# The last two output groups of a set-attention and expert kernel are written into transposed-input tiles, under a new order table

## The chip, the cores and the metric

The kernel runs on one core of one Trainium2 chip. The metric is device time of one launch in microseconds (us). Five engines work side by side, each through its own queue in order: TensorE (PE in the profile, with its weight loads as PEld), VectorE (DVE), ScalarE (ACT), GpSimd (POOL) and SyncE (SP), which here issues nearly all DMA transfers. All arrays are float32.

## The reference

Four batches of 11456 tokens of width 128 attend to 32 inducing points, and the tokens then attend to the 32 result rows. The outcome goes through a skip score and an expert layer with a top-1 gate.

```python
def mab(q, kv):
    s = scale * (q @ kv.transpose(0, 2, 1))
    s = s - s.max(-1, keepdims=True)
    a = np.exp(s)
    a /= a.sum(-1, keepdims=True) + 1e-09
    return a @ kv
h = mab(I, x)
out = mab(x, h)
...
e_idx = np.argmax(logits, axis=1)
...
h = np.maximum(xc[mask] @ w1[e], 0.0)
y[mask] = gate_w[mask, None] * (h @ w2[e])
...
out[do_compute] = xc + y
```

Inputs: x (4, 11456, 128), inducing (32, 128), w_skip (128), w_gate (128, 8), w1 (8, 128, 1024), w2 (8, 1024, 128).

## The kernel before, in words

A batch is cut into six groups: five of 2048 tokens and one of 1216 (batch 0 has the short one first). A group lies as four streams of up to 512 tokens, so that the 32 inducing points times four streams fill 128 partitions.

Each batch has two passes and a middle. The **first pass** (`first`) loads a group of x (channels by tokens) over SP, multiplies it by the inducing points (L372), takes running maxima on DVE (L378) and exponentials on ACT (L382), transposes x into token-major tiles `xt` by 128x128 blocks (L407; four blocks a set, copied out of PSUM by ACT at L335 or DVE at L337), transposes the exponentials (L391) and sums the weighted tokens (L417, accumulated at L426). There are two `xt` tiles, each [128, 4, 4, 129] with a column of ones; the first passes of all batches take them in turn. The **middle** makes the 32 rows h of the batch (`hr`, its transpose `hc`, L486 to L512), finds the expert that they go to, fetches that expert's weights over SP (L665, L667: `w1s`, `w2s`), and folds them with h into `yr` (L590, L603, L643, L654). The **second pass** (`second`) scores tokens against `hc` (L693), turns the scores over on DVE (L698), takes maxima (L700), subtracts them (L704), exponentiates (L707), sums (L711), normalises (L716), turns back (L721, `u1`), makes gate values and scales by them (L820, `v`), and turns back again (L721, `u2`). The elementwise steps L704, L716 and L820 may run on POOL or on DVE; a copy out of PSUM may run on ACT or DVE.

`emit` ends a group. It multiplies `u1` by `hr` and `u2` by `yr` into four PSUM banks (L872), copies the four banks into two tiles named `o` of [128, 2, 512] (`stream`, L335 on ACT or L337 on DVE), and SP stores each `o` tile (`store`, L882). There are four `o` tiles in turn: a copy into one waits until its earlier store has landed. At the end of each batch `marking` checks that no token went elsewhere (`lo`, `lom`, `lod`, `lon`, L903 to L936), and `judge` (L957 to L962) joins the marks of all batches into `anyi`, which SP and the other engines read last of all; a further branch for other experts is skipped with these inputs.

The order of all work on all engines comes from a planner that runs when the program is built: each step has a cost for each engine that may run it, the steps and buffers that it needs, and a rank. The table `PLACES` gives each step, by three characters, its rank (two characters) and a surcharge for DVE (one). From these `in_order` picks the next step, its engine and its PSUM bank, and so fixes every engine's queue. In names such as `x_3_4` or `u2_3_4` the first number after the name is the batch, the second the group (0 to 5).

Of the kernel before, what the change touches and what calls it, by code (L numbers as in the profile page):

```python
# [139 lines left out]
def best_order(ops, bufs):  # L140
# [16 lines left out]
    "0f0AP0Cb2913E30CG0D_2ER1CP0FX2E50Aq0Bp09S06v3An07603G42-0AB0Dk0Bm06m0AC0BA04r0BD3Cr38I05N02U4CK02R04013S2Ee05v0AZ06p39B0"
    "9l02f0Aj01s04G0640FB0Cm04c06a0AA3D-46F0Ef0Di09G0Al07X03r2AX01A01x03F33A06J07M20Z02L04o03T02k09o02v00F04k32s15J04h04Q00R0"
    "C603X01N05H03a06800X28M02B04D2BI08_02b08E09001u0AM05K0693BM07I0CY01v46h1Bi0BL4Eu1DJ09k0GX06-07x08t0AD0AV0780EU04X0DL0FS0"
    "6w07u06r13z0AI3DA07e0Cf0Ad0BX07q39-0El04d0Cc02c03803O01q06i02Y19F08R18P07z35u08p14_06s0BB09t0E20440Bf06U2B407H3AR0C54820"  # L160
    "Bx35B08D08S0Fx00o03305C0660D402l27Q07C38N0DO2Cz01X3CL02303k03o0EY06Y0E_07J0Ff05z22_03R0BY05x03v05Z3370FP27D0AJ02100L01Z0"
    "0J05I00l22D0723Ao01K0Dh00x44J02r00601p01n01202T02d01_03205930E03c22X06M02921909v03400-02C02004S24w08H06e01803002504f03D2"
    "1b01W22J07s08l30h08z01130z06g07G01F06y06u09y0BS0A606k42A03p04i23e29h03I17n08O0ES0Cq0GH0D109208q1Be0Bo0FN07m0DS0EE0Da04C0"
    "GG0DT48y0Du0Ae4EB3Cu0Fb3EZ27R0A10E70EW4E40FK0CX4Dd0F809p0GY0DV0Ar0CO0Cl0Cx4Fu2Fl0G409d39s1Fy06246x38u0A-01o08x2A708s0861"
# [981 lines left out]
```

## Time and profile before

| | |
|---|---|
| time before, median of 3 runs | 225.07 us (224.65 to 226.6) |
| profiled execution: its time / its span | 226.54 us / 224.7 us |
| mean granted TensorE clock in it | 0.981 |
| PE busy (matmul) / PEld | 201.1 us (89%) / 116.2 us (52%) |
| DVE / ACT / POOL busy | 170.5 us (76%) / 140.8 us (63%) / 111.0 us (49%) |
| HBM read / written | 27.68 MB / 23.46 MB |

Busy time is the union of an engine's instructions; ends of matmuls are modelled, so a busy PE may hide short stalls. The span runs from the first to the last instruction that the profiler saw, and the run's own time is a little longer. The chain of waits is followed back from the last instruction to what released it.

### The profile page before, as it was taken

The numbers are of one execution on the slowest core, as the hardware profiler recorded it, in microseconds if no ns is written. First come the engines' busy times: TensorE is split into PE (matmuls) and PEld (weight loads), VectorE is DVE, ScalarE is ACT, GpSimd is POOL, SyncE is SP. The second block draws the span as 40 slices with busy tenths as digits, with TensorE's granted clock in tenths as the row PEclk, the third lists the DMA queues.
The fourth block names the chain that finished last, engine by engine and source line by source line (L and its number), as shares of the span: only waits on it lengthen the run. The fifth ranks groups of instructions, "written<-read, shape, count | busy, mean of one in ns | idle before, by whom it ended". The sixth has DMA issues, their size and how long they took to land.

```text
span 224.7 us, 6693 instructions
## 1 busy us (share of the span) xinstructions
PE 201.1 (89%) x2541; PEld 116.2 (52%) x2542; DVE 170.5 (76%) x444; ACT 140.8 (63%) x333; POOL 111.0 (49%) x284
## 2 busy tenths in 40 slices
PE   4899999989999999999999999989999979688630
PEld 1556767657368764543675647327585333233210
DVE  4363653659898997799888787989898989997640
ACT  2356476655598886766996864768785756346730
POOL 7000000222538668457366541357677879989610
PEclk9999999999999999999999999999999999999975
DMA  6999970086796027979993492454221867445692
GB/s 160 378 419 405 412 313 13 6 266 203 248 392 239 3 115 249 297 308 355 370 414 150 190 314 98 141 234 190 93 101 42 330 205 285 190 175 198 252 365 71
DMA packets 16614, 51.64 MB, mean 230 GB/s; under 512 B 1984, under 2 KB 4928, under 8 KB 16576
## 3 DMA queue, kind: packets, MB, share of 16 engines
q1 hardware_dynamic: 16288, 51.12, 61.4%
q8 instruction: 22, 0.36, 0.7%
q14 instruction: 16, 0.13, 0.2%
q10 hardware_dynamic: 288, 0.02, 0.1%
HBM read 27.68 MB, written 23.46 MB: 228 GB/s over the span
## 4 chain that ended last, share of the span: by engine, by line
PE 54%; POOL 11%; DVE 11%; DMA 10%; ACT 5%; issue 4%; SPq 1%; DVEq 0%; ACTq 0%; POOLq 0%
PE bank L407 16%; PE bank L872 12%; PE bank L417 8%; PE bank L372 6%; DMA w1s<-in_w_dram 4%; PE bank L391 3%; DMA x<-in_xT_dram 3%; ACT o L335 3%; PE bank L693 3%; DMA out_dram<-o 3%; POOL e L716 2%; POOL v L820 2%; DVE ts L700 2%; DVE e L698 2%; PE bank L778 2%
## 5 line engine op out<-in xcount | busy, mean ns | idle before, releaser
L407 PE MATMUL bank<-ident,x 128*128 128x128 f32 (+1 forms) x368 | 50.8, 281 | 1.0 <-DMA x<-in_xT_dram 0.8
L335 ACT COPY o<-bank 128x512 f32<-128x512 f32 (+1 forms) x80 | 40.9, 570 | 16.4 <-PE bank L872 14.4
L335 ACT COPY xt<-bank 128x512 f32<-128x512 f32 (+1 forms) x78 | 42.9, 591 | 10.9 <-PE bank L407 10.6
L704 POOL TENSOR_TENSOR e<-e,ts 128x512 f32<-128x512 f32 (+1 forms) x22 | 22.5, 1023 | 49.6 <-DVE cmx L536 37.5
L407 PEld LDWEIGHTS bank<-ident,x 128*128 128x128 f32 (+1 forms) x368 | 40.4, 141 | 12.7 <-issue 3.0
L872 PE MATMUL bank<-u,hr 32*128 32x512 f32 (+1 forms) x192 | 26.0, 608 | 3.4 <-ACT o L335 2.5
L716 POOL TENSOR_TENSOR e<-texp,ts 128x512 f32<-128x512 f32 (+1 forms) x19 | 18.9, 999 | 17.0 <-DVE ts L713 13.0
L820 POOL TENSOR_TENSOR v<-e,gs 128x512 f32<-128x512 f32 (+1 forms) x20 | 20.8, 1040 | 8.9 <-DVE gs L337 4.9
L417 PE MATMUL bank<-xt,a1T 128*32 128x129 f32 (+1 forms) x736 | 25.1, 275 | 0.0
L382 ACT ACTIVATE a<-bank,bias 128x512 f32<-128x512 f32 (+1 forms) x24 | 16.0, 666 | 14.5 <-DVE a L378 14.5
L372 PE MATMUL bank<-x,iT_sb 128*32 128x512 f32 (+1 forms) x192 | 24.8, 583 | 0.0
L872 PE MATMUL bank<-u,yr 32*128 32x512 f32 (+1 forms) x192 | 23.9, 565 | 0.7 <-DVE u L721 0.6
L417 PEld LDWEIGHTS bank<-xt,a1T 128*32 128x32 f32 (+1 forms) x736 | 19.3, 109 | 8.1 <-issue 3.8
L693 PE MATMUL bank<-x,hc 128*32 128x512 f32 (+1 forms) x192 | 22.8, 573 | 0.1
L707 ACT ACTIVATE texp<-e 128x512 f32<-128x512 f32 (+1 forms) x24 | 14.6, 609 | 10.9 <-POOL e L704 8.0
L378 DVE TENSOR_SCALAR_CACHE_REDUCE a<-bank,bias 128x512 f32<-128x512 f32 (+1 forms) x20 | 13.9, 693 | 5.5 <-PE bank L372 5.2
L698 DVE STREAM_TRANSPOSE e<-bank 128x512 f32<-128x512 f32 (+1 forms) x24 | 15.9, 664 | 2.1 <-PE bank L693 2.0
L721 DVE STREAM_TRANSPOSE u<-v 128x512 f32<-128x512 f32 (+1 forms) x24 | 15.9, 664 | 1.7 <-POOL v L820 1.6
L721 DVE STREAM_TRANSPOSE u<-e 128x512 f32<-128x512 f32 (+1 forms) x24 | 15.6, 661 | 1.1 <-POOL e L716 0.9
L700 DVE TENSOR_REDUCE ts<-e 128x16 f32<-128x512 f32 (+1 forms) x24 | 15.7, 653 | 0.8
L711 DVE TENSOR_REDUCE sums<-texp 128x16 f32<-128x528 f32 (+1 forms) x24 | 15.6, 648 | 0.9 <-ACT texp L707 0.9
L872 PEld LDWEIGHTS bank<-u,yr 32*128 32x128 f32 x192 | 9.8, 185 | 10.8 <-issue 5.8
(153 smaller groups left out, 293.9 us busy)
## 6 DMA issues: line engine op xcount, KB each, us to landing
x<-in_xT_dram SPq DMA_DIRECT2D x43, 512.0 KB, 8.1
out_dram<-o SPq DMA_DIRECT2D x40, 512.0 KB, 3.9
out_dram<-o SPq DMA_DIRECT2D x8, 304.0 KB, 4.7
w1s<-in_w_dram SPq DMA_DIRECT2D x4, 512.0 KB, 4.2
w2s<-in_w_dram SPq DMA_DIRECT2D x4, 512.0 KB, 4.9
x<-in_xT_dram SPq DMA_DIRECT2D x4, 152.0 KB, 2.8
x<-in_xT_dram SPq DMA_DIRECT2D x3, 96.0 KB, 9.1
iT_sb<-in_iT_dram ACTq DMA_DIRECT2D x1, 16.0 KB, 2.2
```

The source lines that it names most:

```text
L335: nc.scalar.copy(out=out, in_=in_)
L372: nc.tensor.matmul(ps[q * M:(q + 1) * M, 0:W], lhsT=iT_sb, rhs=s.x[g][:, G.s1[q]:G.s1[q] + W], start=True, stop=True)
L407: nc.tensor.transpose(out=px[0:w, q * P:(q + 1) * P], in_=s.x[g][:, o:o + w], identity=ident)
L417: nc.tensor.matmul(ph[q * M:(q + 1) * M, 0:P + 1], lhsT=st["aT"][0:w, i, q * M:(q + 1) * M], rhs=xts[bx.idx][0:w, i, q, :], start=(i == 0) ...
L693: nc.tensor.matmul(ps[q * M:(q + 1) * M, 0:W], lhsT=s.hc[:, 0:M], rhs=x()[:, G.s2[q]:G.s2[q] + W], start=True, stop=True)
L698: nc.vector.transpose(out=t[:, 0:W], in_=st["ps"][:, 0:W])
L700: nc.vector.tensor_reduce(out=mx[:, 0:nb], in_=blocks(t), axis=AX.X, op=ALU.max)
L704: on(o).tensor_tensor(out=blocks(t), in0=blocks(t), in1=wide(st["mx"]), op=ALU.subtract)
L716: on(o).tensor_tensor(out=blocks(st["e"]), in0=ev(M), in1=wide(st["i"]), op=ALU.mult)
L721: nc.vector.transpose(out=st[f"u{k}"][:, 0:W], in_=st[src][:, 0:W])
L820: on(o).tensor_tensor(out=blocks(u), in0=blocks(st["e"]), in1=wide(st["gm"]), op=ALU.mult)
L872: nc.tensor.matmul(bank(bp[q].idx)[:, 0:G.w1], lhsT=m[r, :], rhs=st[k][r, c], start=(k == "u1"), stop=(k == "u2"))
```

## The change

It has two parts. In the last batch, the last two groups in number (g = 4 and g = 5) no longer take `o` tiles: group 4 copies its four banks into `xt1` and group 5 into `xt0`, each seen as two halves of 1024 columns, and the stores read from there. These two groups neither take nor free an `o` buffer in the planner. And every character of `PLACES` is replaced, so that every queue stands in another order and some steps run on another engine. All computed operations and their sizes stay.

```diff
 PLACES = (
-    "6f04O07A08w08i07W4EO0Au2CN0BE07Z09L0CF0Dj0GS0Fj04V0BK09N0881AW0BU0EL06z4Fr0FV37b0As0BP02a06H00304q02F06Q05F23V01Q18B0603"
...
+    "Db08q0CS0Bv0G30Gr4GD0A839f0GL3GT0ES0FC09y07X08R0Bl06P09E0DY45904H43K04x12Y0A_14A03e23H05s04d07Z02w04l02Z03t46y04G0A403O4"
...
+        late = b == B - 1 and NG - g <= BUFS["xt"]
+
         def stream(o, q):
-            if q % 2 == 0:
+            if late:
+                v = xts[NG - 1 - g].rearrange("p i q c -> p (i q c)")
+                t[q // 2] = v[:, q // 2 * (GC // 2):(q // 2 + 1) * (GC // 2)].rearrange("p (q w) -> p q w", q=2)
+            elif q % 2 == 0:
                 t[q // 2] = wk.tile([P, 2, GC // Q], F32, tag="o", bufs=BUFS["o"], name=f"o_{b}_{g}_{q // 2}")
             copy(o, t[q // 2][:, q % 2, 0:G.w1], bank(bp[q].idx)[:, 0:G.w1])
...
-            o = L.add({**act(G.w1), **dve(G.w1)}, lambda o, q=2 * h: stream(o, q), m, o, take=[bo], free=[bp[2 * h]])
+            o = L.add({**act(G.w1), **dve(G.w1)}, lambda o, q=2 * h: stream(o, q), m, o, take=[] if late else [bo], free=[bp[2 * h]])
             p = L.add({**act(G.w1), **dve(G.w1)}, lambda o, q=2 * h + 1: stream(o, q), o, free=[bp[2 * h + 1]])
-            L.add({"SP": 0.08}, lambda o, h=h: store(o, h), o, p, free=[bo], size=G.cols * 0.256)
+            L.add({"SP": 0.08}, lambda o, h=h: store(o, h), o, p, free=[] if late else [bo], size=G.cols * 0.256)
```

The diff adds five lines to `emit`, so lines after it carry numbers five higher in the changed kernel.

**The end of the two copying engines.** ACT's last rows before the final reads, with tile numbers (`o_3_4_0` is the first half of batch 3, group 4):

```order
L335 COPY o_3_2_1_3145<-bank1_71 128x512
L748 ACTIVATE gexp2_119<-gexp2_119 128x2x5x8
L335 COPY o_3_4_0_3174<-bank7_77 128x512
L335 COPY lod_3_3178<-bank1_71 128x1
L335 COPY o_3_4_0_3174<-bank3_73 128x512
L335 COPY o_3_4_1_3190<-bank6_76 128x512
L335 COPY o_3_5_0_3205<-bank3_73 128x304
L335 COPY o_3_5_0_3205<-bank1_71 128x304
L335 COPY o_3_5_1_3210<-bank5_75 128x304
```

and in the change:

```order
L335 COPY xt1_165<-bank1_71 128x512
L748 ACTIVATE gexp2_119<-gexp2_119 128x2x5x8
L335 COPY o_3_1_0_3172<-bank4_74 128x512
L335 COPY o_3_1_0_3172<-bank7_77 128x512
L335 COPY o_3_1_1_3181<-bank5_75 128x512
L335 COPY o_3_1_1_3181<-bank0_70 128x512
L335 COPY lod_3_3193<-bank1_71 128x1
L335 COPY xt0_164<-bank7_77 128x304
L335 COPY xt0_164<-bank4_74 128x304
L335 COPY xt0_164<-bank2_72 128x304
```

The fourth copy of groups 4 and 5 stood on DVE before; in the change only group 5 has one copy on DVE, and group 1 takes the place of group 4 as the last full group. On DVE that copy moves ahead of the two steps of `judge`. Before:

```order
L721 STREAM_TRANSPOSE u2_3_5_3188<-v2_3_5_3180 128x320
L928 TENSOR_REDUCE marks_116<-lon_3_3184 128x1
L337 COPY o_3_4_1_3190<-bank4_74 128x512
L960 TENSOR_SCALAR two_180<-bank4_74 128x8
L962 TENSOR_REDUCE anyi_181<-two_180 128x1
L337 COPY o_3_5_1_3210<-bank7_77 128x304
```

and in the change:

```order
L721 STREAM_TRANSPOSE u2_3_5_3179<-v2_3_5_3176 128x320
L337 COPY xt0_164<-bank6_76 128x304
L933 TENSOR_REDUCE marks_116<-lon_3_3197 128x1
L965 TENSOR_SCALAR two_180<-bank6_76 128x8
L967 TENSOR_REDUCE anyi_181<-two_180 128x1
```

**POOL behind the last middle.** POOL's rows after the expert of batch 3 is known, before:

```order
L921 TENSOR_SCALAR lod_2798<-lod_2798 128x1
L923 TENSOR_TENSOR lon_2816<-gmax,lod_2798 128x8
L924 TENSOR_TENSOR lon_2816<-lon_2816,gabs 128x8
L925 TENSOR_SCALAR lon_2816<-lon_2816 128x8
L716 TENSOR_TENSOR e_3_0_2712<-texp_135,ts_3_146 128x512
L806 TENSOR_TENSOR lt_4_2697<-lt_4_2697,gs_2_162 128x64
L704 TENSOR_TENSOR e_3_1_2758<-e_3_1_2758,ts_4_147 128x512
L820 TENSOR_TENSOR v_2_4_2854<-e_2_4_2484,gs_2_163 128x512
L704 TENSOR_TENSOR e_3_2_2828<-e_3_2_2828,ts_0_139 128x512
L921 TENSOR_SCALAR lod_2874<-lod_2874 128x1
```

and in the change:

```order
L937 TENSOR_SCALAR gxs<-gxs 128x96
L938 TENSOR_TENSOR gxs<-gxs,posm 128x96
L704 TENSOR_TENSOR e_3_1_2745<-e_3_1_2745,ts_4_147 128x512
L716 TENSOR_TENSOR e_3_0_2717<-texp_135,ts_3_146 128x512
L704 TENSOR_TENSOR e_3_2_2809<-e_3_2_2809,ts_0_139 128x512
L765 TENSOR_TENSOR gs_2_163<-gs_2_161,gs_2_162 128x10
L820 TENSOR_TENSOR v_2_5_2859<-e_2_5_2598,gs_2_163 128x320
L716 TENSOR_TENSOR e_3_1_2745<-texp_136,ts_4_148 128x512
```

Before, the blocks of four `lod`/`lon` steps of batches 2 and 1 both stand between the score steps of batch 3; in the change the block of batch 1 is done earlier and that of batch 2 comes near the end, and the short group of batch 2 (`v_2_5`) stands where a full one (`v_2_4`) stood.

**PE in batch 1.** Twelve rows of PE where batch 0 is in its second and batch 1 in its first pass, before:

```order
L391 MATMUL bank_77<-ident,a_1_3_668 128x128 x4
L407 MATMUL bank_73<-ident,x_3_412 128x128 x4
L372 MATMUL bank_72<-x_5_490,iT_sb 32x304 x4
L407 MATMUL bank_77<-ident,x_3_412 128x128 x4
L407 MATMUL bank_73<-ident,x_3_412 128x128 x4
L372 MATMUL bank_76<-x_0_683,iT_sb 32x512 x4
L463 MATMUL bank_77<-ident,bias_5_948 1x128
L407 MATMUL bank_73<-ident,x_3_412 128x128 x4
L407 MATMUL bank_72<-ident,x_4_480 128x128 x4
L474 MATMUL bank_77<-ones,mn_974 32x1 x4
L407 MATMUL bank_71<-ident,x_4_480 128x128 x4
L417 MATMUL bank_73<-xt_165,a1T_3_913 32x129 x16
```

and in the change:

```order
L417 MATMUL bank_77<-xt_165,a1T_3_772 32x129 x16
L407 MATMUL bank_73<-ident,x_4_472 128x128 x4
L391 MATMUL bank_72<-ident,a_1_4_817 128x128 x4
L407 MATMUL bank_74<-ident,x_4_472 128x128 x4
L811 MATMUL bank_73<-lt_1_909,rep 32x16 x4
L407 MATMUL bank_70<-ident,x_4_472 128x128 x4
L407 MATMUL bank_75<-ident,x_5_482 128x128 x4
L407 MATMUL bank_73<-ident,x_5_482 128x128 x4
L417 MATMUL bank_70<-xt_164,a1T_4_1012 32x129 x16
L407 MATMUL bank_75<-ident,x_5_482 48x128 x4
L407 MATMUL bank_73<-ident,x_0_611 128x128 x4
L407 MATMUL bank_72<-ident,x_0_611 128x128 x4
```

Sets of transposes (L391, L407) alternate with products in strips of 32 in both; in the change more of them stand in runs.

## Rows read from the trace of the kernel before

**Rows 1.** The page, part 1: busy us of an engine, its share of the span, instructions.

```profile
PE 201.1 (89%) x2541; PEld 116.2 (52%) x2542; DVE 170.5 (76%) x444; ACT 140.8 (63%) x333; POOL 111.0 (49%) x284
```

**Rows 2.** Busy time by stretches: the stretch, its length, then busy us of PE, PEld, DVE, ACT and POOL, the granted TensorE clock, the DMA share and GB/s.

```profile
10.00:178.00 168.00, 164.53 (x2196) 100.43 (x2200) 133.28 (x352) 116.14 (x275) 75.81 (x171) 1.00 0.62 230
...
178.00:204.00 26.00, 21.15 (x236) 8.18 (x228) 23.62 (x60) 13.47 (x33) 22.72 (x54) 1.00 0.56 214
...
40.00:176.00 136.00, 133.16 (x1801) 78.80 (x1803) 116.93 (x314) 96.47 (x232) 73.97 (x166) 1.00 0.59 213
```

**Rows 3.** The chain of waits, its last pieces: start, length, what.

```profile
211.28 6.30 DMA out_dram<-o
...
217.70 0.47 DVE o L337
```

**Rows 4.** Waits over the whole run: who waited for whom, us in total, times, longest.

```profile
ACT o L335 <- DMA out_dram<-o: 1.4, 1, 1.4
...
PE bank L590 <- DMA w1s<-in_w_dram: 1.8, 3, 1.1
...
DVE o L337 <- DMA out_dram<-o: 1.1, 1, 1.1
```

**Rows 5.** The timeline of ACT and DVE at the end: start, length, engine, line, operation, and in brackets the idle time before it with its releaser.

```profile
216.44 0.16 DVE L962 TENSOR_REDUCE anyi<-two 128x1 int32<-128x8 f32 x1
217.70 0.47 DVE L337 COPY o<-bank 128x304 f32<-128x304 f32 x1 [1.10 <-DMA out_dram<-o]
...
215.54 0.73 ACT L335 COPY o<-bank 128x304 f32<-128x304 f32 x2 [1.27 <-PE bank L872]
217.68 0.41 ACT L335 COPY o<-bank 128x304 f32<-128x304 f32 x1 [1.41 <-DMA out_dram<-o]
```

**Rows 6.** The last microseconds by stretches, columns as in rows 2.

```profile
217.00:218.00 1.00, 0.00 (x0) 0.00 (x0) 0.30 (x1) 0.32 (x1) 0.00 (x0) 0.50 0.98 381
218.00:219.00 1.00, 0.00 (x0) 0.00 (x0) 0.17 (x1) 0.09 (x1) 0.00 (x0) 0.50 0.91 317
219.00:220.00 1.00, 0.00 (x0) 0.00 (x0) 0.00 (x0) 0.00 (x0) 0.00 (x0) 0.50 0.92 294
220.00:221.00 1.00, 0.00 (x0) 0.00 (x0) 0.00 (x0) 0.00 (x0) 0.00 (x0) 0.50 0.24 70
```

**Rows 7.** The store that ends the program, in the timeline, and the DMA issues from 217 us on with their us to landing.

```profile
218.24 0.38 SPq L882 DMA_DIRECT2D out_dram<-o  x1
...
out_dram<-o SPq DMA_DIRECT2D x1, 304.0 KB, 4.1
```

**Rows 8.** The timeline of PE at two places, start first: how long a set takes is the distance to the next start.

```profile
20.11 1.04 PE L372 MATMUL bank<-x,iT_sb 128*32 128x512 f32 x8
21.08 0.66 PE L391 MATMUL bank<-ident,a 128*128 128x128 f32 x4
...
23.54 1.07 PE L372 MATMUL bank<-x,iT_sb 128*32 128x512 f32 x8
24.43 1.83 PE L417 MATMUL bank<-xt,a1T 128*32 128x129 f32 x60
...
109.57 1.09 PE L407 MATMUL bank<-ident,x 128*128 128x128 f32 x8
110.50 0.60 PE L391 MATMUL bank<-ident,a 128*128 128x128 f32 x4
...
113.21 1.09 PE L407 MATMUL bank<-ident,x 128*128 128x128 f32 x8
114.24 1.09 PE L417 MATMUL bank<-xt,a1T 128*32 128x129 f32 x32
```

**Rows 9.** The timeline of POOL before and behind the last middle: start, length, line, operation.

```profile
175.80 0.73 POOL L820 TENSOR_TENSOR v<-e,gs 128x320 f32<-128x320 f32 x1
...
177.64 0.45 POOL L932 TENSOR_SCALAR gxs<-gxs 128x96 f32<-128x96 f32 x1
178.17 0.39 POOL L933 TENSOR_TENSOR gxs<-gxs,posm 128x96 f32<-128x96 f32 x1
...
182.11 0.19 POOL L921 TENSOR_SCALAR lod<-lod 128x1 f32<-128x1 f32 x1
...
183.16 1.05 POOL L716 TENSOR_TENSOR e<-texp,ts 128x512 f32<-128x512 f32 x1
184.17 0.35 POOL L806 TENSOR_TENSOR lt<-lt,gs 128x64 f32<-128x64 f32 x1
```

**Rows 10.** Waits from 178 us on: DVE for POOL.

```profile
DVE u L721 <- POOL v L820: 1.0, 3, 0.5
...
DVE u L721 <- POOL e L716: 0.9, 2, 0.5
```

**Rows 11.** Groups of DVE by line and shape: count, busy us, mean ns.

```profile
L337 DVE COPY xt<-bank 128x512 f32<-128x512 f32 x13 | 8.7, 679 | 3.1 <-PE bank L407 3.1
L337 DVE COPY o<-bank 128x512 f32<-128x512 f32 x11 | 7.3, 673 | 1.5 <-PE bank L872 1.4
...
L820 DVE TENSOR_TENSOR v<-e,gs 128x512 f32<-128x512 f32 x3 | 2.0, 681 | 0.0
```

**Rows 12.** The timeline of DVE and POOL where both do an elementwise step on SBUF.

```profile
82.76 1.70 POOL L820 TENSOR_TENSOR v<-e,gs 128x512 f32<-128x512 f32 x1 [1.07 <-ACT gs L335]
82.88 0.67 DVE L820 TENSOR_TENSOR v<-e,gs 128x512 f32<-128x512 f32 x1
```

More of the change, by code (lines that the diff above doesn't have):

```diff
@@ L157 @@
[L157 to L164, printed above, removed]
@@ new lines @@
+    "6v06u23L07O08c0A103A06903X0Cr0720C035w09G3BF09r07l03W3AF02p25F07A0Cy07C0DU0EW0Cz0EP1FF0E12Fq0Ae2E80GU4Ct0DP1CZ0FB07p05y0"
+    "6-08L05Z04f13C03w16O03c16Q03G43B03U03507R02E02702P00201O01500y01X01n11R01311f01600X20p00C01400z00800u00v12a00k01p00M01l0"
+    "0P01700L30m00T20F00501c10N00t00731C01v00000300900x00I00Z00132600H00a00w30A01841s00J0D304-08127e04g09a3Ab06104s09P05Y0B60"
+    "B408Z0Dt0Cx43_04j0EJ34e3Aw05626A03205J04U06g26309l04422U03703002502F05A03j03l07a36p16003Y03h13k16d05E44p23409x05g04V43y0"
@@ new lines @@
+    "BT0Bf13P04y0D40Eu08O0DI0AZ0Dk05x47W4CF03i0Bs49B1CM07t25a3Dl0Cq06W0El0AW0EH0Dy0CV0EQ0C20GA08p0E90D90Cp0CN3B04AP0Dm0BI4Ce0"
+    "ET03z19W2AE07706i03p19K04E0BC3Fi06N0Dv06S07Q07x08X09t03a09R09H0650AX2DD08t04D45G17v0Ax0Dc03S09X05L0B_49q08C0AH0Bp09607M0"
+    "Bh06b06a2BK08345d0Eh16Y07J24709u15S02902M00V00l01V00B00R30W00j10601W40s01I01z01Q40K00i05b07i05508v0BA0Eb1480AO1CJ07526x0"
+    "F53Ad0An38E0D603f03102t03b0CH04k15W02z33T03m31h06T05u05Q28G06s0AT05R06U04O0420Ed4CG08a1C70As3BW05e4460CD4A508J0Fy0EM09T0"
@@ new lines @@
+    "8y08u0Af2A-07T1Ck0DK4DA0FH0G705h00G02O00U01b03I01j00_01T02031L01E42G01o01U02D00o00b01e00Y00n02C30e00h02J02o00d01F00-0110"
+    "0g00c25P03Z0Do1570AL0Ah27h03x05B06H08I0CU02s0C40AA1Bc08z08B0Ez2Fc1DZ04R1BS3BX04P0CP0FV44S05m0513580A005i0Cn04u09i0AQ0DJ0"
+    "6t38H18g0BQ0B909F34h08M09325H0AR04Z05p29-08F08w07z08k02c02y07S09o08x05T06D16M03r02h0AC08N2Et06z44N2760AJ0Gf0804Fu0Bb0FJ1"
+    "AS0Ew0Ag0Be0840E308Y0ER0Ay2Bo17m0B308o1CR3Ff0CW2DM2Es07904L0CC28D06209k1DX0F10At0DF0C60660FR0Ch07u0Ak4Cg0Cf0C519Y36m06h0"
@@ new lines @@
+    "Dd48_04K06f03R22m02v03q24n03g02f01k04I02r05l02d02l04r04104Q43N33d03n33912n09J08e0820FN0FL0By2Fn07E0Dq09Z08807U04m06V07_1"
+    "6F03-32j03F39804C15r05V0AK07f06E09O0Bm08j0Fm0Em19m04w12q07814305I4D509w2E206L0A704i06l07N04z0AI45C05t0450Cc3Aq08n39505O3"
+    "9n07005-04a06k06J04M04J19S09c34X05n25U08m22x03v06e06n0D70Dp07F0Ai09V09b06w0Br1Dz0AD2Ee0Co3DT05N17o0B709109e03o0Bi09A07D4"
+    "7H0Bg43u0CL05v0F84Bw0Dr02e02302K01i02I03E03Q03M02X12g01-11q02B01042T00E01901w02V02801t41d00Q01A01J01Z02202S01x22H0244AG0"
@@ L181 @@
+    "BL3D80G005K0EV3900Ea0G83F60G50EC0Au0EE0D00EU0DC0EY27g0Df0D-17b0CK0Ec09N1Du07B06C04q1FI09Q02k38W08P0CT07K05z09z0Am09d05j0"
+    "990EK0DL08r15M09738537n02u0A30Ap15D07V0Bn1CA0E60En0890Cv0BN0DE09M0Bd2FT07q0G21Bz17P0Bj4Ev27I0Gd0Gn0H04Gb0Gu0H22Go0G_0H80"
+    "GB0Gw0Gk0FG0HA0GZ0G-0Gs0Gz2G42GY0GW4Fs2H40HB0Gy0H30HD0HE0H92HF0HC0HG0H60H50"
 )
```

27 lines of the change are left out of this document (8 added, 19 removed).

## The prediction, made before the changed kernel was run

> **What bounds the kernel now.** I read the page's busy shares first, then stretches of the run, then the end of the chain of waits, then the rows around it. The shares name PE, at 89% [rows 1]. The stretches show that this holds for one part of the run only. From 10 to 178 us PE is busy 164.5 of 168 us, DVE 133 and ACT 116 [rows 2]: PE sets the pace, and 3.5 us at most can be won by filling its gaps. From 178 to 204 us PE drops to 21.2 of 26, while DVE has 23.6 and POOL 22.7 [rows 2]: here the second pass of batch 3 goes from POOL to DVE and back, and each waits for the other. The last part belongs to the stores. The chain ends with a transfer of 6.30 us and then a copy of 0.47 us into the tile that this transfer had held [rows 3]. ACT waited 1.4 us and DVE 1.1 us for that landing, each once in the whole run [rows 4].
>
> So three stretches have three limits: PE's queue, the pair of POOL and DVE, and the `o` tiles with the stores behind them.
>
> **The end.** The last store is issued at 218.24 us and lands after 4.1 us [rows 7]. Without the wait, ACT's third copy of 304 columns follows the two that start at 215.54 and take 0.73, so it runs from 216.27 to 216.7 instead of from 217.68. DVE's copy would start when `anyi` is made, at 216.60, and end at 217.07 instead of 218.17 [rows 5]: 1.1 us earlier. In the changed order this copy also stands ahead of `judge`, so that ACT's copy ends last, at 216.7: 1.5 us earlier. Against this stands the traffic. From 217 us on the transfers still move 381, 317, 294 and 70 GB/s in successive microseconds [rows 6], 1.06 MB; at the 381 of the first they need 2.8 us where they took about 3.6. If the pipe is the limit, only 0.8 is won. I take **-1.1**, with -0.8 and -1.5 as ends. The copies themselves keep their sizes. The new tiles are free by then: their last readers, the weighted sums of batch 3 (L417), stand before the middle of batch 3 on PE. That leaves no price for them.
>
> **PE before 178 us.** The two orders have the same products before the first score product on `hc_3`, but not the same neighbours. Two sets of transposes take 0.93 us when transposes follow (109.57 to 110.50) and 1.03 when a product in strips of 32 follows (113.21 to 114.24). A strip product of 512 columns takes 0.97 when transposes follow (20.11 to 21.08) and 0.89 when strips follow (23.54 to 24.43) [rows 8]. A run of transposes therefore costs 0.10 at its end and 0.08 before it. Counting PE's rows in both orders up to that point, transposes (L391, L407) stand in 53 runs before and in 48 now; one place of it is shown with the change. Five runs by 0.18 make **-0.9**, all of it on PE, which is the bound there. The ends are 0, where other engines hold PE up, and -1.5.
>
> A page of the Trainium skill speaks against this term: Perfetto Trace Analysis, section Identifying the Most-Contended Engine, says that matmul busy time is a poor measure for PE and that weight loads are to be looked at instead. Those are busy 52% [rows 1], less than DVE's 76%, so by that page DVE is the engine to save on, the term is nothing, and the sum below is -1.6 in place of -2.5. I keep the term, since between 10 and 178 us PE has hardly a gap that waits for DVE.
>
> **The second pass of batch 3.** From the first score step of batch 3 on, POOL loses the two blocks of `lod`/`lon` (182.11 to 183.16, so 1.05 each), one L806 (0.35) and a full `v` of batch 2 (as long as the L716 of 1.05). It gets the two `gxs` steps (0.45 and 0.39) and a short `v` (0.73) [rows 9]. That is 3.5 less and 1.6 more, so -1.9. One block returns near the end, ahead of the last group's gate step, which must wait for DVE there anyway. DVE's list between `hc_3` and the last turn has 86 instructions in both orders, with nearly the same sum. What the relief can give is bounded by DVE's waits for POOL after 178 us: 1.0 and 0.9 [rows 10]. I take **-0.5**, about a quarter, because the chain changes hands every microsecond; the ends are -1.9 and 0.
>
> **What DVE takes over.** Four more full `v` steps (0.681 each) and, net, three more `xt` copies (0.679) come to DVE; three full `o` copies (0.673) leave it [rows 11]. L704 gets two and L716 loses two of about the same length. Together this is about +2.7 us. DVE idles 19 of the 136 us between 40 and 176 us [rows 2], and PE covers the rest, so I take **0**; if that cover is gone it costs +2.7.
>
> **SP and the stalls of the new order.** SP now issues the first load of batch 2 ahead of the weights of batch 0. PE waited 1.8 us in all for weights [rows 4]; the load starts while the address of the expert is still being worked out, so it should be over before the weights start. I take 0. Which other gaps open or close cannot be read off an order: PE's 3.5 us of gaps [rows 2] could shrink by some 2 or double. I take 0, with -2 and +3.5 as ends.
>
> **Sum.** -1.1 - 0.9 - 0.5 = -2.5 us. The profiled execution took 226.54 us, 1.8 more than its span; it becomes 224.0. The median of the runs is 225.07, 1.5 below the profiled one, and the same step gives **222.6 us**, 1.1% less.
>
> **Rivals.**
> *The gain stays at the end.* PE's switches are hidden behind waits for copies, and the relief of POOL is eaten by DVE, so only 0.8 of the end is left. For it speaks that the stores move at near 400 GB/s for the last stretch, and that PE's gain is small against its gaps; against it, that PE has so few gaps. 225.07 - 0.8 = 224.3 us. Chance 0.32.
>
> *The wait only moves.* Group 1 still takes `o` tiles, those of group 3, and could wait for its stores as group 5 did for those of group 2. But two groups lie between them now, where only one did. It gives back 1.1: 223.7 us. Chance 0.04.
>
> *DVE becomes the bound.* Before, a `v` on DVE beside a `v` on POOL stretched POOL's step to 1.70 us, against 1.05 alone [rows 9, 12]. Three more such two-input steps now run on DVE. At 0.65 each POOL loses 2.0, and DVE has its 2.7 more. If they fall where PE already waits for `u`, -1.1 - 0.9 + 2.7 + 2.0 = +2.7, which is 227.8 us. The point from which it decides is the use of DVE in the second passes of batches 0 to 2: once it has no idle time there, every added step is paid. Against it stand the 19 us of idle time. Chance 0.15.
> The rule behind it is in the Trainium skill, SBUF — State Buffer, section Who interferes with whom: a DVE instruction with two inputs in SBUF and a GpSimd instruction that reads SBUF shut each other out for a whole instruction. The pair of rows at 82.8 us agrees.
>
> **Numbers.** A run of this kernel can be told from no change from about 1% on. The chances are 0.46 for the forecast, 0.32, 0.04 and 0.15 for the rivals, and 0.03 for stalls that I do not see. As the forecast lies just over 1%, 0.04 of its 0.46 falls within it: faster by over 1% 0.42, within 1% 0.40 (0.04 + 0.32 + 0.04), slower 0.18 (0.15 + 0.03). The range reaches down to 219.0, where the better ends of the stores, the transposes and POOL's relief (-1.5, -1.5, -1.9) meet 1.2 us of PE's gaps, and up to 227.0, which takes in the first two rivals and the nearer part of the third; the rest of the third and what lies below are the 2 in 10 that are left out.
>
> **What would show it.** ACT's and DVE's waits for the landing of a store are gone, and the last store is issued 1.1 to 1.5 us sooner behind the last turn of `u2`. PE's busy time up to the first L693 of batch 3 falls by about 1 us with gaps as before. From there to the last `u2` the time is 0.5 us shorter, with fewer waits of DVE for POOL. I would be wrong if PE's gaps before that point grow by more than 2 us, if POOL's `v` steps are stretched on the way to PE, or if the last store still waits behind a full pipe.

## The result and the profile after

| | before | changed |
|---|---|---|
| median of 22 runs each | 225.69 us (223.48 to 227.34) | 227.25 us (225.94 to 228.6) |
| ratio, 95% interval | | 1.0071 (1.0049 to 1.0094) |
| profiled execution: its time / its span | 226.54 / 224.7 us | 228.6 / 226.8 us |

The change makes the kernel 0.7% slower: 1.6 us between the medians. The profiled execution of the changed kernel is the longest of its 22 runs, that of before is 0.85 above its median, so the two traces differ by 2.06, somewhat more than the medians.

The page of the changed kernel, part 1, to be read beside [rows 1]:

```profile
PE 202.7 (89%) x2541; PEld 117.2 (52%) x2542; DVE 176.8 (78%) x448; ACT 140.1 (62%) x332; POOL 108.1 (48%) x281
```

PE's share is still 89%, so this line does not show what happened. Stages do. The cuts are the first score product (L693) on `hc` of each batch, then the end of the last `u2` (L721), then the end. Busy time by stages of the changed kernel, columns as in [rows 2]:

```profile
40.22:92.58 52.36, 51.02 (x686) 32.61 (x679) 45.88 (x120) 37.05 (x89) 25.02 (x59) 1.00 0.57 205
92.58:140.10 47.52, 45.61 (x634) 27.94 (x636) 39.14 (x102) 33.46 (x80) 22.98 (x53) 1.00 0.70 259
140.10:179.70 39.60, 36.96 (x494) 19.86 (x485) 36.73 (x93) 27.56 (x69) 23.57 (x54) 1.00 0.40 146
179.70:217.65 37.95, 31.49 (x329) 13.12 (x326) 33.68 (x87) 21.31 (x51) 31.73 (x73) 1.00 0.64 244
217.65:226.80 9.15, 1.39 (x10) 0.82 (x10) 0.87 (x4) 1.11 (x5) 0.83 (x4) 0.57 0.53 191
```

The same stages of the kernel before:

```profile
40.23:88.27 48.04, 46.87 (x668) 30.02 (x667) 40.09 (x113) 32.63 (x82) 24.41 (x62) 1.00 0.55 187
88.27:137.39 49.12, 48.64 (x625) 27.22 (x624) 43.01 (x113) 37.00 (x86) 26.50 (x55) 1.00 0.82 299
137.39:175.90 38.51, 37.32 (x507) 21.40 (x506) 33.70 (x88) 26.52 (x66) 22.96 (x50) 1.00 0.36 136
175.90:214.63 38.73, 30.91 (x328) 12.77 (x327) 33.49 (x86) 22.28 (x54) 32.99 (x80) 1.00 0.60 231
214.63:224.70 10.07, 1.18 (x10) 0.61 (x10) 1.66 (x6) 1.14 (x3) 0.13 (x1) 0.59 0.54 198
```

Work moves between the first three stages, so only their sum can be compared: `hc_3` comes at 179.70 instead of 175.90, **3.80 us later**. From there to the last `u2` the changed kernel takes 0.78 less (37.95 against 38.73), and from there to the end 0.92 less. That is +2.1. The loss is made before batch 3 begins its second pass, and both later stages gain. How large it is in a usual run is told below by a second pair of traces: it is nearer 2.5 than 3.8.

Is it work or waiting? Between `hc_0` and `hc_3` PE's idle time, the length of a stage less its busy time, grows from 2.8 us (1.17, 0.48, 1.19) to 5.9 (1.34, 1.91, 2.64). Some waiting hides in rows that count as busy, so I also gave every row of PE there the distance to the next row's start that is usual for its line, its shape and the kind of row behind it (the lower fifth over the traces). These distances add up to 127.2 us before and 126.9 in the change. What is left over is **8.5 us before and 12.6 in the change**. This is an estimate: with the rows grouped in three other ways the growth of what is left over is 3.1 to 3.7 in place of 4.1, and PE's own work grows by 0.1 to 0.8. In each of them most of the loss is waiting. The waits of PE from 41 to 180 us, changed kernel (who waited for whom, us in total, times, longest):

```profile
PE bank L590 <- DMA w1s<-in_w_dram: 2.2, 2, 1.2
PE bank L811 <- POOL lt L806: 0.7, 2, 0.5
PE bank L590 <- ACT o L335: 0.6, 1, 0.6
PE bank L730 <- ACT hc L335: 0.6, 1, 0.6
PE bank L486 <- ACT gs L335: 0.5, 1, 0.5
PE bank L463 <- ACT a L382: 0.4, 1, 0.4
```

and before, from 41 to 176 us:

```profile
PE bank L590 <- DMA w1s<-in_w_dram: 1.6, 2, 1.1
PE bank L778 <- DVE u L721: 0.4, 1, 0.4
PE bank L811 <- POOL lt L806: 0.3, 1, 0.3
```

The 0.6 of L590 for ACT is batch 2's; before, the same row waited 0.56 for its weights. Three of the new waits stand one behind the other on the last stretch to `hc_3`. The timeline of PE there, changed kernel:

```profile
171.68 0.26 PE L811 MATMUL bank<-lt,rep 128*32 128x16 f32 x8 [0.51 <-POOL lt L806]
...
175.71 0.49 PE L486 MATMUL bank<-acc,rep 128*128 128x129 f32 x2 [0.51 <-ACT gs L335]
...
178.06 0.33 PE L503 MATMUL bank<-ident,hr 128*128 128x128 f32 x1
179.00 0.77 PE L730 MATMUL bank<-u,lr 32*32 32x160 f32 x16 [0.61 <-ACT hc L335]
179.70 1.06 PE L693 MATMUL bank<-x,hc 128*32 128x512 f32 x8
```

and before:

```profile
172.62 0.49 PE L486 MATMUL bank<-acc,rep 128*128 128x129 f32 x2
...
174.97 0.33 PE L503 MATMUL bank<-ident,hr 128*128 128x128 f32 x1
175.90 1.06 PE L693 MATMUL bank<-x,hc 128*32 128x512 f32 x8
```

Before, the row that needs `hc_3` comes 0.93 behind L503; in the change L730 stands between them and itself waits, so it is 1.64. Against the usual distances the three places cost 0.68, 0.55 and 0.71, or 1.94 together. Two more stand earlier: PE waits for the weights of batch 1, which cost nothing there before, 1.41 over the usual, and for the bias row of batch 2 (L463) 0.59:

```profile
98.63 0.64 PE L590 MATMUL bank<-w1s,hc 128*32 128x256 f32 x8 [1.20 <-DMA w1s<-in_w_dram]
...
115.52 0.27 PE L463 MATMUL bank<-ident,bias 128*1 128x128 f32 x1 [0.42 <-ACT a L382]
```

Together that is 3.94 of the 4.1 of this estimate; the other differences nearly cancel. At the end no engine waits for a store any more ([rows 4] had two such waits). After 217 us, changed kernel, the last turn, the copies, the end of `judge` and the issue of the last store:

```profile
217.13 0.51 DVE L721 STREAM_TRANSPOSE u<-v 128x320 f32<-128x320 f32 x1
218.60 0.47 DVE L337 COPY xt<-bank 128x304 f32<-128x304 f32 x1 [0.95 <-PE bank L872]
...
218.51 1.04 ACT L335 COPY xt<-bank 128x304 f32<-128x304 f32 x3 [0.79 <-PE bank L872]
...
220.03 0.16 DVE L967 TENSOR_REDUCE anyi<-two 128x1 int32<-128x8 f32 x1
...
219.75 0.44 SPq L887 DMA_DIRECT2D out_dram<-xt  x1
```

The last `u2` ends at 217.64 and the last store is issued at 219.75, 2.1 behind it, where it was 3.6 before (218.24 in [rows 7] less 214.63). It lands after 4.0 us, at 223.8, which is 6.1 behind the last `u2`, where it was 7.7 before (222.36). So the last store comes 1.5 us sooner and lands 1.6 sooner, but the program ends only 0.92 sooner. Behind the landing the change takes 3.0 us and before took 2.4. What stands there is the branch over the other experts, which every engine takes when it has read `anyi`. Instructions of that line, changed kernel (count, then ns, then first and last start):

```profile
L975 SPq EVENT_SEMAPHORE  x9: 17/17/17, 224.8 to 225.4; - x9
...
L975 SPq COMPARE_BRANCH  x1: 53/53/53, 221.2 to 221.2; - x1
```

SP branches at 221.2 and goes on at 224.8, a microsecond after the last store has landed. The change puts DVE's last copy ahead of `judge`, POOL's last `lon` is done only just before that copy ends (218.9), and `anyi` is now made 2.5 us behind the last `u2` (220.19), where it was 2.0 (216.60).

### The profile page after: what moved, and what is told of

It reads as the page before. It is cut to its first block, busy times and chain, and to the rows that moved or that the text cites. A ratio compares the mean times of both kernels' runs of the same rounds, so it can differ in the third digit from the quotient of the medians.

```text
span 226.8 us, 6691 instructions
## 1 busy us (share of the span) xinstructions
PE 202.7 (89%) x2541; PEld 117.2 (52%) x2542; DVE 176.8 (78%) x448; ACT 140.1 (62%) x332; POOL 108.1 (48%) x281
## 4 chain that ended last, share of the span: by engine, by line
PE 61%; DVE 13%; POOL 12%; DMA 4%; issue 3%; ACT 3%; SPq 0%; POOLq 0%; DVEq 0%
PE bank L407 15%; PE bank L872 12%; PE bank L372 9%; PE bank L417 9%; PE bank L391 5%; DMA w1s<-in_w_dram 4%; PE bank L693 3%; POOL v L820 3%; DVE u L721 2%; POOL e L716 2%; POOL e L704 2%; PE bank L778 2%; DVE e L698 1%; DVE sel L243 1%; DVE ts L700 1%
## 5 line engine op out<-in xcount | busy, mean ns | idle before, releaser
L335 ACT COPY xt<-bank 128x512 f32<-128x512 f32 (+2 forms) x82 | 44.1, 583 | 14.1 <-PE bank L407 12.8
L407 PE MATMUL bank<-ident,x 128*128 128x128 f32 (+1 forms) x368 | 50.3, 282 | 0.0
L335 ACT COPY o<-bank 128x512 f32<-128x512 f32 (+1 forms) x77 | 39.6, 572 | 11.4 <-PE bank L872 10.8
L407 PEld LDWEIGHTS bank<-ident,x 128*128 128x128 f32 (+1 forms) x368 | 41.0, 142 | 10.6 <-issue 3.8
L704 POOL TENSOR_TENSOR e<-e,ts 128x512 f32<-128x512 f32 (+1 forms) x21 | 21.1, 1004 | 45.8 <-DVE ts L700 45.8
L716 POOL TENSOR_TENSOR e<-texp,ts 128x512 f32<-128x512 f32 (+1 forms) x21 | 21.3, 1014 | 19.5 <-DVE ts L713 14.7
L872 PE MATMUL bank<-u,hr 32*128 32x512 f32 (+1 forms) x192 | 26.1, 611 | 2.5 <-ACT o L335 1.4
L872 PE MATMUL bank<-u,yr 32*128 32x512 f32 (+1 forms) x192 | 23.9, 563 | 0.2 <-DVE u L721 0.2
L693 PE MATMUL bank<-x,hc 128*32 128x512 f32 (+1 forms) x192 | 23.3, 571 | 0.0
L820 POOL TENSOR_TENSOR v<-e,gs 128x512 f32<-128x512 f32 (+1 forms) x16 | 15.8, 987 | 5.8 <-DVE gs L337 2.8
L337 DVE COPY xt<-bank 128x512 f32<-128x512 f32 (+1 forms) x18 | 12.0, 673 | 6.0 <-PE bank L407 4.1
L721 DVE STREAM_TRANSPOSE u<-v 128x512 f32<-128x512 f32 (+1 forms) x24 | 16.0, 668 | 0.8 <-POOL v L820 0.5
L721 DVE STREAM_TRANSPOSE u<-e 128x512 f32<-128x512 f32 (+1 forms) x24 | 15.8, 663 | 0.4 <-POOL e L716 0.2
```

The lines of the kernel that those rows point to most:

```text
L335: nc.scalar.copy(out=out, in_=in_)
L407: nc.tensor.transpose(out=px[0:w, q * P:(q + 1) * P], in_=s.x[g][:, o:o + w], identity=ident)
L693: nc.tensor.matmul(ps[q * M:(q + 1) * M, 0:W], lhsT=s.hc[:, 0:M], rhs=x()[:, G.s2[q]:G.s2[q] + W], start=True, stop=True)
L704: on(o).tensor_tensor(out=blocks(t), in0=blocks(t), in1=wide(st["mx"]), op=ALU.subtract)
L716: on(o).tensor_tensor(out=blocks(st["e"]), in0=ev(M), in1=wide(st["i"]), op=ALU.mult)
L721: nc.vector.transpose(out=st[f"u{k}"][:, 0:W], in_=st[src][:, 0:W])
```

## The experiments

In these kernels the planner is replaced by a list `PLAN` of steps with their engines and a list of PSUM banks. Written so, the two orders give the instruction streams of the kernel before and of the change. The list fixes the order of every queue, the engine of every step and the PSUM banks, so "order" means all three. Lines up to `emit` stand 64 lower there: L629 is L693, L526 is L590, L808 is L872. "Tiles" is the use of `xt` for the last two groups. Ratios are to the kernel before on the same chip, with 95% intervals.

**Tiles and order apart.** The first kernel has before's order and the new tiles, the second the new order and `o` tiles everywhere:

```diff
-        o.rank, o.spare = 64 * r + d, SPARES[e]
+        o.eng = ENGINES[int(PLAN[i + 2])]
...
+        late = b == B - 1 and NG - g <= BUFS["xt"]
```
```diff
-        late = b == B - 1 and NG - g <= BUFS["xt"]
+        late = False
```

> Every queue in the order of before, step by step and bank by bank; only the last two groups of batch 3 copy into xt tiles. Theory 1 (the new tiles gain at the end, the new order loses ahead of hc_3): the stretch from the last u2 (214.63) to the end, 10.07 us before and 9.15 in the changed kernel, shrinks by about 0.9, so 224.8 against a before of 225.7; no wait of ACT or DVE for a store. Theory 2 (the stores were the limit anyway): 225.7, the last store issued sooner and landing as late.

Measured (e1): 0.9982 (0.9954 to 1.001); 225.44 against 225.95 us, an interval that takes in no change.

> The changed kernel in its own order, step by step, but with o tiles for all groups again: the other half of e1. If the tiles are worth the predicted 1.1 us in this order, 228.3 against the changed kernel's 227.25, with a wait of ACT or DVE for a store near the end. If they are worth what e1 measured (0.4 us, 0.74 in the profile's end), 227.7. If nothing, 227.25.

Measured (j1): 1.0097 (1.0059 to 1.0136); 228.16 against 226.1 us. Its trace is of a run at its median (228.09), where that of the change was the longest of 22. The row that needs `hc_3`, order alone (j1) and tiles alone (e1):

```profile
178.34 1.06 PE L629 MATMUL bank<-x,hc 128*32 128x512 f32 x8
```
```profile
175.84 1.06 PE L629 MATMUL bank<-x,hc 128*32 128x512 f32 x8
```

So in this pair the new order brings `hc_3` 2.5 us later, in place of 3.8. PE's plain idle time from `hc_0` on is 5.1 against 2.8 (5.9 against 2.8 in the first pair). The tail takes 38.0 (38.9 in e1), the end 9.95. The end waits for a store again, longer than the kernel before ever did:

```profile
218.48 0.47 DVE L273 COPY o<-bank 128x304 f32<-128x304 f32 x1 [2.14 <-DMA out_dram<-o]
```

So the loss belongs to the order: about 2.1 us by the medians, and by the traces all of it ahead of `hc_3`. What the tiles give is not clear of noise: 0.5 us by the medians of the first kernel, and 0.0026 between order alone and the change, whose intervals meet. In the traces they take away a wait of 2.14 and give back about 0.8 (9.95 against 9.15 behind the last `u2`). The last store lands 6.2 us behind the last `u2` in order alone and 6.1 in the change; what comes sooner is `anyi`, 2.5 behind it in place of 3.7, since `judge` stands behind DVE's waiting copy.

**Head and tail apart.** Order of before up to `hc_3`, then the new order and tiles; the new order up to `hc_3`, then that of before with `o` tiles; and the first again with a mended seam. The lists are strings of codes, so the edit is told in short:

```diff
-PLAN = before
+PLAN = before[:hc_3] + [s for s in changed if s not in before[:hc_3]]
```

> The order of before up to the first score product on hc_3 (175.90 us before, 179.70 in the changed kernel), and from there the order of the changed kernel with its tiles; the two sets of steps done by then differ in 19 of 1105. Theory 1 (the loss of 3.8 lies ahead of hc_3, tail and end gain 0.8 and 0.9): 225.7 - 1.7 = 224.0. Theory 2 (the gain of tail and end in the profile comes from what the slow head left done, or from chance): 225.7 or more. If DVE's share of work in the tail were what costs, over 226.

Measured (e2): 1.0135 (1.0111 to 1.0159). `hc_3` came at 176.92, but behind it the seam put the marks of batch 1 in front, PE stood still for 2 us, and its clock fell. Windows from 178 us on, columns as in [rows 2]:

```profile
178.00:180.00 2.00, 0.03 (x1) 0.04 (x1) 1.15 (x6) 1.15 (x4) 1.21 (x6) 1.00 0.35 141
180.00:182.00 2.00, 1.96 (x24) 0.80 (x24) 1.93 (x5) 0.75 (x3) 1.29 (x3) 0.85 0.39 156
182.00:184.00 2.00, 2.00 (x12) 1.00 (x16) 1.90 (x6) 0.63 (x1) 1.71 (x5) 0.50 0.31 115
184.00:186.00 2.00, 2.00 (x16) 0.29 (x12) 1.97 (x4) 0.66 (x2) 1.67 (x7) 0.80 0.70 199
```

> The changed order up to the first score product on hc_3, then the order of before, with o tiles for all groups. Theory 1 (the head loses 3.8, and nothing is won behind it): 225.7 + 3.8 = 229.5, down to 228 if the profiled run of the changed kernel (228.6 against its median of 227.25) overstated the loss. Theory 2 (the head costs nothing, the loss is made up in some runs): about 225.7 to 226.5. Theory 3 (the new steps left over at hc_3 matter, not the head): under 227.

Measured (e3): 1.0244 (1.0219 to 1.027). Here too the seam spoiled it: the step from `hr_3` to `hc_3` took 4.0 us instead of 1.64. Neither of the two decides anything on head or tail.

> e2 without its own fault at the seam (there the marks of batch 1 stood in line on PE, DVE, ACT and POOL right at hc_3, DVE waited 1.84 us for them, PE 1.98, and PE's granted clock fell to half for about 4 us): order of before up to hc_3, then that of the changed kernel, and the four late steps of batch 1's marks near the end. Theory 1 (the whole loss lies ahead of hc_3; tail and end of the changed order gain 0.8 and 0.9): hc_3 at 175.9, last u2 38.0 later, 9.2 to the end, so 225.5 - 1.6 = 223.9. Theory 2 (the tail of the changed order is only faster from what its own head leaves): 225 or more.

Measured (h1): 1.0103 (1.006 to 1.0146). In its trace (226.41 us, against a median of 228.40) `hc_3` comes at 175.51, the end takes 9.21, but the stretch between takes 39.94. In this splice the new order's tail does not gain, and the tail of e3, before's order behind the new head, takes 38.56. The 38.0 of the new order is seen only behind its own head. Whether that comes from what the head leaves over or from the seams is not shown, so head and tail are not priced apart here.

**Engines.** The change also gives 86 of the 1105 steps to another engine: by the two lists 67 copies change between ACT and DVE, and 19 steps of the second passes between POOL and DVE. First comes the new order with these 19 back on the engines of before (the expectation counts 20); then, in before's order with new tiles, four full `v` steps moved from POOL to DVE, or seven copies of the first passes from ACT to DVE; then the reverse of each in the changed kernel.

```diff
-L756 POOL TENSOR_TENSOR v_1_2<-e_1_2,gs_0 128x512
+L756 DVE TENSOR_TENSOR v_1_2<-e_1_2,gs_0 128x512
...
-L273 ACT COPY a1T_1_4<-bank_77 128x512
+L273 DVE COPY a1T_1_4<-bank_77 128x512
```

> The changed kernel with its order, but each elementwise step L704, L716, L820 and each small gate copy of the second pass on the engine that before gave it (20 of them change; DVE's elementwise steps fall from 14 to 11, its v from 8 to 4). Theory 1 (PE stands in front of things that are not ready: weights of batch 1, a bank at 112 us, the middle of batch 3 at 170 to 179 us; who makes v does not matter): within 0.5 of the changed kernel, 226.8 to 227.8. Theory 2 (DVE's added steps and the stretch they cause, DVE busy 176.8 us against 170.5, set the loss): 2 us faster, near 225.3.

Measured (e4): 1.0235 (1.021 to 1.026), DVE busy 173.4. PE found new or longer waits (L811 for POOL 1.9 in all, `hc` of batch 2 for DVE 1.2, a bias row for ACT 1.1), `hc_3` at 182.62.

> e1 (order of before, new tiles) with four full v steps (batches 1 and 2) on DVE instead of POOL, as the changed kernel has them. Theory 1 (PE covers what DVE gets more, the prediction's 0): 225.2 to 225.6, as e1. Theory 2 (DVE's added work and its two-input steps beside POOL's hold PE up): 2 to 4 us more, 227.5 or over.

Measured (h2): 1.0012 (0.9995 to 1.0029), 0.3% over the tiles alone, with intervals that meet: no cost is shown.

> e1 with seven copies of the first passes (four xt, three a1T, batches 1 to 3) on DVE instead of ACT, which the changed kernel has there: 0.68 each, 4.8 us of DVE. The prediction left the three a1T out of its sum. Theory 1 (covered by PE): 225.2 to 225.6. Theory 2 (DVE's load sets the head): 226.5 to 229.

Measured (h3): 1.0126 (1.0102 to 1.015): 1.4% over the same kernel without the move, some 3 us for 4.8 us of copies. PE now waits for DVE in places where it did not:

```profile
111.97 1.97 PE L343 MATMUL bank<-ident,x 128*128 128x128 f32 x16 [0.30 <-DVE a1T L273]
...
124.58 0.66 PE L343 MATMUL bank<-ident,x 128*128 128x128 f32 x4 [0.52 <-DVE xt L273]
```

> The changed kernel with the same seven copies of first passes (four xt, three a1T) on ACT instead of DVE, everything else in its place; DVE falls by 4.8 us, ACT, busy 140 us, gets 4.1. Theory 2 of h3 (copies on DVE hold PE up: there they cost 3.0 us): 1 to 3 us less than the changed kernel's 227.25, 224.5 to 226.2. Rival (in the changed order ACT is at work just then, as its trace shows at all seven, so that the copies only wait elsewhere): 227.25 or more.

Measured (i1): 1.0169 (1.0136 to 1.0201), clear of the changed kernel's 1.0071 (1.0049 to 1.0094); DVE busy down to 172.2 and ACT up to 143.3.

> The changed kernel with the four full v steps of batches 1 and 2 back on POOL, as before had them. By h2 (the four cost 0.4 to 0.7 us on DVE in the old order) 0.5 less, 226.7. Rival, by e4 (20 steps given back cost 4 us: the order counts on v being done in 0.68 instead of 1.05 us): 228 or more.

Measured (i2): 1.0107 (1.0074 to 1.0139), with an interval that meets the changed kernel's; DVE 172.7, POOL 111.7.

The seven copies cost time either way: 1.4% when they go to DVE in before's order, 1.0% when they leave it in the new one. For the four `v` steps neither move is clear of noise. So DVE's load by itself does not explain the loss. The other 60 copies that change between ACT and DVE were not given back in any run, so a part of theirs in the loss is not ruled out.

**The named waits.** In the changed kernel, PE's rows are put in another order at the places where it waits: L590 of batch 1 (f1), the bias row of batch 2 (f2), the way to `hc_3` (f3, and in another manner g1), all of them (f4, g2). f3, f4, g1 and g2 also move rows of DVE and ACT there.

```diff
-L526 MATMUL bank_74<-w1s_1,hc_1 32x256 x4
 L343 MATMUL bank_73<-ident,x_2_2 128x128 x4
 L353 MATMUL bank_76<-xt_165,a1T_2_1 32x129 x16
+L526 MATMUL bank_74<-w1s_1,hc_1 32x256 x4
...
+L353 MATMUL bank_77<-xt_165,a1T_3_5 32x129 x12
 L808 MATMUL bank_76<-u1_2_2,hr_2 128x512
...
-L353 MATMUL bank_70<-xt_165,a1T_3_5 32x129 x12
...
+L439 MATMUL bank_70<-ident,hr_3 128x128
 L808 MATMUL bank_76<-u1_2_1,hr_2 128x512
...
-L439 MATMUL bank_74<-ident,hr_3 128x128
```

> The changed kernel with one PE row moved: batch 1's L590 (which waits 1.2 us for its weights at 97.43) goes behind the set of transposes and the L417 that follow it, which are ready. Theory 1 (PE's rows stand in front of things that are not there yet, and each such wait is paid in full): the wait is gone and the time is 1.0 to 1.2 us less than the changed kernel's 227.25, so 226.1. Theory 2 (DVE and ACT set the pace, and the wait only moves to the next row): 227 or more, with new gaps of PE within 20 us behind it.

Measured (f1): 1.005 (1.0029 to 1.0072). The wait of 1.20 is gone, in part because the weights land 0.7 us sooner in this trace, and the next row of that chain, which needs ACT's copy of the product, has one:

```profile
97.73 0.61 PE L526 MATMUL bank<-w1s,hc 128*32 128x256 f32 x8
98.84 0.44 PE L539 MATMUL bank<-ident,g 128*128 128x128 f32 x2 [0.49 <-ACT g L271]
```

> The changed kernel with the L463 of batch 2 (idle 0.42 ahead of it at 115.5, 0.6 against its usual pitch) behind the next set of transposes, and its L474 behind the set after that. Theory 1: 0.4 to 0.6 us less, so 226.7. Theory 2: no change, 227.25.

Measured (f2): 1.0068 (1.0046 to 1.009); nothing to tell from the changed kernel. Its trace also shows that the waits for weights are no fixed price: L590 of batch 1, left in its place here, waits 0.42 in place of 1.20, and that of batch 2 waits 1.38.

> The changed kernel with the rows ahead of hc_3 in another order: the last L417 of batch 3 goes ahead of two groups of L872, its sum on DVE and its scaling on ACT first in line, and the second of these groups stands behind L503, so that PE works while hc_3 is copied. Three waits of PE (0.51, 0.51, 0.61 us at 171 to 179 us) lie there. Theory 1: hc_3's first product comes 1.4 to 1.9 us sooner than 179.7 and the whole is as much shorter, 225.6. Theory 2 (POOL and DVE set the pace from 165 us on): hc_3 is sooner, but the last u2 is not, 227 or more.

Measured (f3): 1.0302 (1.0258 to 1.0347). My own order was at fault: PE waited 3.3 us for one copy on ACT, its clock fell, and the products behind it ran slowly. Windows, columns as in [rows 2]:

```profile
178.00:180.00 2.00, 2.00 (x16) 0.68 (x12) 1.18 (x4) 0.10 (x1) 0.65 (x2) 0.59 1.02 408
180.00:182.00 2.00, 2.00 (x27) 0.66 (x19) 0.00 (x0) 1.05 (x3) 0.18 (x1) 0.55 0.18 70
```

> The three edits of the runs before in one kernel. Theory 1: the sum, 3.0 to 3.6 us less than the changed kernel, so 223.9, and 0.8% below the kernel before. Theory 2: less than 1 us is won, 226.3 or more, since DVE is as busy as it was.

Measured (f4): 1.0309 (1.0275 to 1.0343), for the same reason.

> The edit of f3 done again without its own fault (there L503 waited 3.26 us for its bank, and DVE's normalising of hr_3 stood behind a sum that waited 1.90 for ACT): L503 and the last L417 of batch 3 get banks that are free, and hr_3 comes first on DVE and hc_3's copy first on ACT. Of the three waits of PE ahead of hc_3 (pitch 0.68, 0.55, 0.71 us over its usual one in every run of the changed order so far) the last two should go. Theory 1 (a wait of PE ahead of hc_3 is paid in full): 1.0 to 1.3 us less than the changed kernel's 227.25, so 226.1, as the delay of f3 was paid in full. Theory 2 (the wait moves to the next row that needs DVE or POOL, as in f1 and f2): 226.8 or more.

Measured (g1): 1.0042 (1.0023 to 1.006). `hc_3` came at 177.85, 0.5 sooner than with the order alone, but no sooner than in f2 (177.82), where the way to it is as in the change. Two of the waits were replaced by others on the same way:

```profile
174.50 0.33 PE L439 MATMUL bank<-ident,hr 128*128 128x128 f32 x1 [0.43 <-DVE hr L435]
177.15 0.77 PE L666 MATMUL bank<-u,lr 32*32 32x160 f32 x16 [0.40 <-ACT o L271]
```

> g1 with the edits of f1 and f2. Theory 1: f1 gave 0.4 and f2 nothing, so 1.4 to 1.7 less than the changed kernel, 225.7, level with the kernel before. Theory 2: 226.6 or more.

Measured (g2): 1.0056 (1.0035 to 1.0077). Waits that add up to 3.9 us in the longest run's trace give back 0 to 0.3% of the time, at most 0.7 us by the medians, when PE's rows are put so as to avoid them, singly or all at once. The intervals of f1, f2, g1 and g2 all meet that of the changed kernel, so no gain is shown.

**A version that might beat both.** Before's order with the new tiles, and two sets of transposes put ahead of L590 of batch 0:

```diff
+L343 MATMUL bank_70<-ident,x_1_2 128x128 x4
+L343 MATMUL bank_77<-ident,x_1_2 128x128 x4
 L526 MATMUL bank_74<-w1s_0,hc_0 32x256 x4
```

> The order of before with the new tiles (e1), and one PE row moved: two sets of transposes of x_1_2 go ahead of batch 0's L590, which waits 1.05 us for its weights in that order. Theory 1 (paid in full): e1's 225.44 less 0.9, so 224.5. Theory 2 (the wait moves on): 225.2 to 225.5.

Measured (g3): 0.9994 (0.9972 to 1.0016). No better than the tiles alone, which are themselves level with the kernel before.

## Why the prediction was wrong

The forecast was 222.6 us with a range to 227.0; the median is 227.25. Of these 4.65 us, 0.6 lie in the base: the median of 3 runs before was 225.07, that of 22 is 225.69. The rest is a change of +1.6 where -2.5 was forecast. Step by step:

**The end, -1.1.** The waits for stores are gone and the last store is issued 1.5 us sooner, as forecast. The end came as -0.9 between the traces and -0.8 against order alone, inside the ends of the term; by the medians it is 0.5 to 0.6 and not clear of noise. That this is near the -0.8 that I had named for a full pipe is luck: the last store landed 1.6 sooner behind the last `u2`, so the pipe did not hold it back. I had taken the landing of the stores for the end of the program, and DVE's copy ahead of `judge` for a gain only. In the change the path runs from that copy (and the `lon` that ends with it) through `judge` to `anyi`, the branch and the 3.6 us behind it.

**PE before 178 us, -0.9.** This is the step that failed. The sum over rows gives -0.3 for PE's own work in place of -0.9 (0.1 to 0.8 more work in the other groupings), and its waits grew by 4.1 (8.5 to 12.6). I had written that I would be wrong if PE's gaps before that point grew by more than 2 us, and this is what came: by the plain gaps it is 2.8 to 5.9 between `hc_0` and `hc_3`, and 2.8 to 5.1 in the pair of tiles alone and order alone. I had read "hardly a gap" as a sign that little can go wrong there. But the old trace shows the gaps of the old order, and says nothing of those that a new one opens.

**SP and the stalls of the new order, 0.** The second failed step, and the same mistake seen from the other side. The growth of PE's waits was this term: 2.3 us by the plain gaps of the second pair, 3.1 by those of the first and 4.1 by the estimate over rows, against an upper end of +3.5. Setting it to 0 because it could not be read from an order gave the forecast its sign. I had looked at the weights of batch 0 alone; in the change SP issues a group's four loads of `x` right behind those of batch 1. Those weights land after 4.4 us, where it was 3.7 before, which is 0.7 of the wait of 1.20. But the loads are not shown to be the cause: in the traces of f1, f2 and i2, where the same four stand behind the same weights, these land after 3.7, 3.6 and 3.7 us.

**The second pass of batch 3, -0.5.** It came as -0.78 (-0.86 in the second pair), between the ends, and DVE waits 0.5 us for POOL's `v` where it waited 1.0, and hardly for its `e`, where it waited 0.9 [rows 10]. But the cause is not shown: behind before's head nearly the same tail order took 39.9.

**What DVE takes over, 0.** The count was wrong: I missed three more copies of `a1T` and the stretch of `v`. Groups of DVE by shape, changed kernel, then before:

```profile
L820 DVE TENSOR_TENSOR v<-e,gs 128x512 f32<-128x512 f32 x7 | 5.5, 780 | 0.1
L337 DVE COPY a1T<-bank 128x512 f32<-128x512 f32 x6 | 4.1, 684 | 1.1 <-PE bank L391 1.1
```
```profile
L337 DVE COPY a1T<-bank 128x512 f32<-128x512 f32 x3 | 2.1, 688 | 0.6 <-PE bank L391 0.5
```

Between 10 us and `hc_3` DVE has 6.7 us more, not 2.7. That this costs nothing was also wrong as a rule of the kernel before: there, seven copies moved to DVE cost about 3 us. Whether it costs anything in the new order is not shown, since taking the seven copies off DVE made that order slower.

**The rivals.** *DVE becomes the bound* gave 227.8, nearest to the result, but by another mechanism, so its nearness is luck. POOL's `v` did not become longer: 1095 ns before, 1048 now. Against their length alone, its steps lose 1.2 us beside DVE's in the three overlapping pairs of before and 0.6 in the five of the change, where 2.0 more was priced; DVE's lose 1.5 there. With 4.6 us less on DVE (i1) the kernel took longer still; with 4.1 less (i2) it cannot be told from the changed kernel. The Trainium skill (Perfetto Trace Analysis, Identifying the Most-Contended Engine) says to optimize the engine with the highest occupancy first, and to judge TensorE by its share of peak FLOPs or by its weight loads; by the weight loads of [rows 1] that would have been DVE here. These two runs, which moved its work to ACT and POOL, do not bear it out. *The gain stays at the end* had the right size for the end, and no room for a loss elsewhere. *The wait only moves* is not seen: no engine waits for a store.

**What stays open.** Shown are the part (the order, with its engines and banks) and the place (ahead of `hc_3`); the form, waits of PE and little work, rests on its idle time and the estimate over rows. Not shown is a single cause among the other queues. The five named waits hold 3.9 us in the longest run's trace, but moving PE's rows away from them gave at most 0.7 by the medians, and f1 and g1 show PE meeting the lateness of ACT and DVE at the next row instead. Which of their queues makes them late, and whether another choice of engines would mend it, was not settled. No run kept the new order of rows with the old engines of its copies.
